# Converting the FFN weights in other places: four slices in attention, four in MoE, one engine step per f-step in the FFN

## The chip, the cores and the metric

The kernel runs on one core of one Trainium2 chip. The metric is the device time of one execution in microseconds (us), lower is better. The core has five engines that run their own instruction queues: TensorE (PE in the profile; PEld its weight loads), VectorE (DVE), ScalarE (ACT), GpSimd (POOL) and SyncE (SP), which here only issues transfers. ScalarE and GpSimd issue transfers too, from the same queue as their other work. Each queue is worked off in order: an instruction that waits holds everything behind it.

## The reference

Three layers run one after the other on 4 x 448 = 1792 tokens of width 768.

```python
# attention: 12 heads, head_dim 64, heads mixed before and after the softmax
scores = scale * np.matmul(q, k.transpose(0, 1, 3, 2))
scores = np.einsum('bhij,hg->bgij', scores, w_pre)
attn = softmax(scores)
attn = np.einsum('bhij,hg->bgij', attn, w_post)
x = np.matmul(attn, v)            # to (1792, 768)
# MoE: 8 experts, top 1, w1[e] is 768 x 1024, w2[e] is 1024 x 768
out[mask] = gate_w[mask, None] * (np.maximum(x[mask] @ w1[e], 0.0) @ w2[e])
# FFN: w_in is 768 x 2048, w_out is 2048 x 768, both float64
h = x @ w_in
y = (h * (1.0 / (1.0 + np.exp(-h)))) @ w_out
```

The FFN's weights arrive as float64. [...]

## The kernel before

**Float32 by parts.** Every large operand is split into a rounded part and a rest (`rhi`, `rlo` for weights, `xhi`, `xlo` and the like for activations; `split`, `wsplit`). ScalarE casts the first, VectorE subtracts for the second. Three matmuls (`mm3`, lines 798 to 800) then make one product. The split weights live in a ring of four pairs.

**Conversion.** The weights of the FFN are cut into 16 slices (`f`), each 128 x 1536 wide: 768 columns of `w_in`, 768 of `w_out`. A chunk of a slice is loaded as pairs of 32-bit words into a tile `D` and turned into float32 in a tile `CM` in five VectorE operations (mask the high word, add the low word, put in the sign, take out the exponent, multiply) and two ScalarE operations; then `CM` is stored to `w_d[f]` in device memory. The FFN loads slices from there. In attention, slices 0 to 7 are converted, in 48 chunks of 256 columns; in the FFN's first half slices 8 to 15, in 16 chunks of 768 columns.

**Attention** is ordered by a planner (`Plan`): each operation has a due time, a cost and the engines it may run on; a list scheduler writes one queue per engine. Chunk n of the conversion is due at an even share of the 180 groups (lines 648 to 657). SyncE issues all loads, the relay transfers `G<-S` and the conversion's transfers.

**MoE** runs 18 slots of 128 tokens (`slots`). A slot has four matmul steps: two `mm1` (18 matmuls of 512 columns each) and two `mm2` (24 of 384), interleaved with the slot before, so there are 72 steps. Each step splits two weight pairs (`rhi`, `rlo<-wraw`), two steps ahead of TensorE. At a slot's end ScalarE evicts `y` and GpSimd scatters it to `y_d`. `hook(s)` is called with s = a + 2 after slot a; for s = 12, 13, 14 it loads the three x tiles of the FFN's first token group (`xload`), on ScalarE's queue, and for s = 13, 14, 15 it transposes them (`fT`, two calls each).

**FFN.** Five token groups (four of 384 tokens, one of 256), and twice (for slices 0 to 7, then 8 to 15) all groups: 80 f-steps. In f-step n: `s1` (h of one slice; sigmoid on ScalarE, the product `sg` on VectorE, split into `gh`, `gl`), the transposes of the next group's x, `s2` of the f-step before (adds into six PSUM banks), the split of the slice two steps ahead, the load of the slice four ahead, and the conversion. After a group's last slice, `s2` copies the banks into tiles `ob` (two buffers for three tiles of a group) and GpSimd stores them to `p_d`. The next group's x is loaded at its predecessor's first f-step and transposed from the second on. The loads of slices and the conversion's transfers are SyncE's.

In the FFN's conversion a chunk has five steps, one per f-step: load; mask and first ScalarE operation; add and sign; exponent and second ScalarE operation; multiply and store. `D` and `CM` have two buffers; chunk n begins at f-step n x 36 // 16.

Of the kernel before, what the change touches and what calls it, by code (L numbers as in the profile page):

```python
# [9 lines left out]
F32 = mybir.dt.float32  # L10
F32R = mybir.dt.float32r
I32 = mybir.dt.int32
# [19 lines left out]
FH = NF // 2  # L32

# [194 lines left out]
def attention(tc, nc, q, k, v, x_d, oh, cum, zsum, c_e8, ident, wp1, wp2, wg_sb, wf, w_d, bias_e, bias_1):  # L228
    with ExitStack() as st:
# [573 lines left out]
def experts(tc, nc, x_d, y_d, w1, w2, wf, w_d, p_d, bias_e, bias_1, out, ident, oh, cum, zsum, consts,  # L803
# [6 lines left out]
    with outer:  # L810
# [115 lines left out]
        CC = DM  # L926
        wv = wf.bitcast(I32)

        def convert(n, step):
            f, c = FH + n // 2, n % 2 * CC  # L930
            V, A = nc.vector, nc.scalar
            if step == 0:
                tiles["D", n] = gpool.tile([128, CC, 2], I32, name="D", tag="D")
                nc.sync.dma_start(out=tiles["D", n].rearrange("p a b -> p (a b)"), in_=wv[f, :, 2 * c:2 * (c + CC)])
                return
            d = tiles["D", n]
            low, high = d[:, :, 0], d[:, :, 1]
            if step == 1:
                tiles["CM", n] = gpool.tile([128, CC], I32, name="CM", tag="CM")
            m = tiles["CM", n]  # L940
            fl = m.bitcast(F32)
            if step == 1:
                V.tensor_scalar(out=m, in0=high, scalar1=0xfffff, scalar2=None, op0=ALU.bitwise_and)
                A.activation(out=fl, in_=m, func=ACTF.Identity, scale=2.0 ** -20, bias=bias_1)  # L944
            elif step == 2:
                V.scalar_tensor_tensor(out=fl, in0=low.bitcast(U32), scalar=2.0 ** -52, in1=fl, op0=ALU.mult, op1=ALU.add)  # L946
                V.scalar_tensor_tensor(out=m, in0=high, scalar=-(1 << 31), in1=m, op0=ALU.bitwise_and, op1=ALU.bitwise_or)
            elif step == 3:
                V.tensor_scalar(out=high, in0=high, scalar1=20, scalar2=0x7ff,  # L949
                                op0=ALU.logical_shift_right, op1=ALU.bitwise_and)  # L950
                A.activation(out=high, in_=high, func=ACTF.Relu, scale=2.0 ** 23, bias=bias_e)
            elif step == 4:
                V.tensor_tensor(out=fl, in0=fl, in1=high.bitcast(F32), op=ALU.mult)  # L953
                nc.sync.dma_start(out=w_d[f][:, c:c + CC], in_=fl)
# [247 lines left out]
```

## Time and profile before

| | us |
|---|---|
| median of 3 runs (1488.95 to 1495.48) | 1491.22 |
| the profiled execution | 1493.94 |
| its span in the trace | 1492.2 |
| attention, 45 to 555 | 510 |
| MoE, 571 to 945 | 374 |
| FFN, first half with conversion, 945 to 1245.8 | 300.8 |
| FFN, second half, 1245.8 to 1480 | 234.2 |

Busy over the whole span: TensorE 1354.8 us (91%), VectorE 1101.2 (74%), ScalarE 875.8 (59%), GpSimd 507.8 (34%). Such a share is an average over stages with different limits, so the stages are read apart. The granted clock (PEclk) is TensorE's share of full speed in a stretch, 1.00 being 2.4 GHz and 0.50 being 1.2 GHz. In a timeline, `[0.57 <-ACT rhi]` behind a row is the idle time of that engine ahead of the instruction and what ended it. A queue name with q (ACTq, SPq) is the engine's sequencer, which issues transfers.

### The profile page before, as it was taken

What the parts mean: (1) busy time and instruction counts of PE and PEld (TensorE: products, weight loads), DVE (VectorE), ACT (ScalarE), POOL (GpSimd) and SP (SyncE); (2) the same over time, 40 slices, a digit from 0 to 9 for tenths busy, and PEclk for the clock granted to TensorE, in tenths of its full rate; (3) what the DMA queues carried; (4) which work ended last, traced back from release to release, by engine and by line L of the source; (5) the groups of instructions that cost most, each with busy time, mean ns of one, the idle gap of its engine ahead of it and who ended that gap; (6) DMA issues with size and microseconds to landing.
All of it is one profiled execution on the core that took longest, in us unless ns stands there. A gap on an engine that the chain in (4) does not pass through costs nothing. (4 is left out here: it accounts for less than half of the span.)

```text
span 1492.2 us, 24452 instructions
## 1 busy us (share of the span) xinstructions
PE 1354.8 (91%) x8838; PEld 1222.8 (82%) x8838; DVE 1101.2 (74%) x1652; ACT 875.8 (59%) x1500; POOL 507.8 (34%) x613
## 2 busy tenths in 40 slices
PE   4898989899899988999999999898898969999997
PEld 2777878777787877888887889797797959999996
DVE  5999879999898867797887788466566655445554
ACT  3766667777667645777887687444354444343332
POOL 7988668778867742141111110000000000000000
PEclk8999999999999998999999999898999999999998
DMA  7545554654554462179436740555555555355533
GB/s 226 174 154 169 175 171 153 206 179 165 163 166 155 139 200 93 30 268 334 148 121 233 260 154 22 189 189 196 207 188 203 178 203 212 127 190 191 188 132 116
DMA packets 110252, 259.85 MB, mean 174 GB/s; under 512 B 9308, under 2 KB 64896, under 8 KB 110128
## 3 DMA queue, kind: packets, MB, share of 16 engines
q1 hardware_dynamic: 101600, 223.38, 44.9%
q0 software_dynamic: 6512, 29.37, 5.6%
q10 hardware_dynamic: 2016, 5.51, 1.1%
q8 instruction: 71, 1.16, 0.3%
q14 instruction: 53, 0.43, 0.1%
HBM read 254.28 MB, written 36.18 MB: 195 GB/s over the span
## 5 line engine op out<-in xcount | busy, mean ns | idle before, releaser
L850 DVE TENSOR_TENSOR rlo<-wraw,rhi 128x1536 fp32r<-128x1536 f32 x144 | 246.7, 1756 | 63.3 <-ACT rhi L849 62.3
L849 ACT CAST rhi<-wraw 128x1536 fp32r<-128x1536 f32 x144 | 205.0, 1476 | 9.5 <-DMA wraw<-in_moe_w_dram 9.4
L363 POOL TENSOR_TENSOR GL<-G,GH 120x448 fp32r<-120x448 f32 (+1 forms) x164 | 202.3, 1242 | 15.8 <-PE m L799 5.8
L425 PEld LDWEIGHTS m<-WM,E 120*112 120x112 f32 (+1 forms) x1440 | 172.8, 181 | 34.1 <-POOL WM L412 10.2
L425 PE MATMUL m<-WM,E 120*112 120x120 f32 (+1 forms) x1440 | 183.5, 273 | 16.0 <-DVE a_sb L255 5.4
L856 DVE TENSOR_TENSOR rlo<-wf,rhi 128x1536 fp32r<-128x1536 f32 x80 | 140.6, 1758 | 69.3 <-ACT rhi L855 69.3
L798 PE MATMUL b<-fxhi,rhi 128*128 128x384 f32 (+1 forms) x480 | 161.4, 336 | 23.6 <-DVE sg L983 14.6
L800 PE MATMUL b<-fxhi,rlo 128*128 128x384 f32 (+1 forms) x480 | 161.2, 336 | 7.2 <-DVE rlo L856 7.2
L799 PE MATMUL b<-fxlo,rhi 128*128 128x384 f32 (+1 forms) x480 | 160.0, 333 | 0.0
L798 PE MATMUL b<-rhi,gh 128*128 128x384 f32 x436 | 151.0, 346 | 7.6 <-ACT gh L855 4.6
L800 PE MATMUL b<-rhi,gl 128*128 128x384 f32 x436 | 148.6, 341 | 0.0
L799 PE MATMUL b<-rlo,gh 128*128 128x384 f32 x436 | 148.1, 340 | 0.0
L391 ACT ACTIVATE E<-m,mx 120x448 f32<-120x448 f32 x180 | 114.2, 635 | 51.2 <-DVE mx L381 30.0
L381 DVE TENSOR_REDUCE mx<-m 120x1 f32<-120x448 f32 x180 | 109.9, 615 | 18.7 <-PE m L800 18.0
L855 ACT CAST rhi<-wf 128x1536 fp32r<-128x1536 f32 x80 | 118.1, 1478 | 2.0 <-issue 1.3
L798 PEld LDWEIGHTS b<-fxhi,rhi 128*128 128x128 f32 x480 | 93.9, 196 | 25.8 <-DVE sg L983 16.1
L981 ACT ACTIVATE sg<-b 128x384 f32<-128x384 f32 (+1 forms) x80 | 37.2, 465 | 131.4 <-PE b L800 131.3
L906 POOL DMA_INDIRECT y_d<-y,idx_s x18 | 18.3, 1018 | 280.3 <-ACT y L904 244.4
L1012 POOL DMA_DIRECT2D p_d<-ob x14 | 7.7, 550 | 306.1 <-DVE ob L1011 298.8
L983 DVE TENSOR_TENSOR sg<-b,sg 128x384 f32<-128x384 f32 (+1 forms) x80 | 42.3, 529 | 89.5 <-ACT sg L981 89.3
L328 PE MATMUL qkp<-kh,qs 128*120 128x448 f32 (+1 forms) x192 | 84.2, 439 | 23.6 <-DVE qs L319 21.3
L800 PEld LDWEIGHTS b<-fxhi,rlo 128*128 128x128 f32 x480 | 93.8, 195 | 10.0 <-DVE rlo L856 9.8
(196 smaller groups left out, 3420.4 us busy)
## 6 DMA issues: line engine op xcount, KB each, us to landing
wraw<-in_moe_w_dram SPq DMA_DIRECT2D x76, 1536.0 KB
wf<-w_d SPq DMA_DIRECT2D x80, 768.0 KB
G<-S SPq DMA_DIRECT2D x176, 210.0 KB
D<-in_wf_dram SPq DMA_DIRECT2D x48, 256.0 KB
D<-in_wf_dram SPq DMA_DIRECT2D x16, 768.0 KB
rawq<-in_q_dram SPq DMA_DIRECT2D x32, 360.0 KB
raw<-in_k_dram SPq DMA_DIRECT2D x36, 224.0 KB
w_d<-CM SPq DMA_DIRECT2D x48, 128.0 KB
```

Source lines behind the costliest of these rows:

```text
L328: nc.tensor.matmul(p[:m, :S], qs, kh, start=True, stop=False)
L363: G.tensor_tensor(out=t[:n], in0=x[:n], in1=hi[:n].bitcast(F32), op=ALU.subtract)
L381: V.tensor_reduce(out=mx[:n], in_=tiles["m1", i, g][:n, :S], axis=AX.X, op=ALU.max, negate=True)
L391: A.activation(out=t[:n], in_=tiles.pop(("m1", i, g))[:n, :S], func=ACTF.Exp, bias=tiles.pop(("mx", i, g))[:n], accum_out=tiles["z", i, g ...
L425: nc.tensor.matmul(p[:, c, :, :nr], x[:n, c * CH:(c + 1) * CH], wm[:n, :, :nr], start=True, stop=True)
L798: nc.tensor.matmul(p, lh, rh, start=first, stop=False)
L799: nc.tensor.matmul(p, lh, rl, start=False, stop=False)
L800: nc.tensor.matmul(p, ll, rh, start=False, stop=last)
L849: nc.scalar.copy(hi, src)
L850: nc.vector.tensor_tensor(out=lo, in0=src, in1=hi.bitcast(F32), op=ALU.subtract)
L855: nc.scalar.copy(hi, src)
L856: nc.vector.tensor_tensor(out=lo, in0=src, in1=hi.bitcast(F32), op=ALU.subtract)
```

## The change

- Attention converts slices 0 to 3 (`FA = 4`): 24 chunks of 256 columns instead of 48.
- MoE converts slices 4 to 7 with a new class `Convert`: 16 chunks of 384 columns, from matmul step 24 on, chunk n beginning n x 42 // 16 steps later.
- The FFN converts slices 8 to 15 with the same class: 16 chunks of 768 columns, chunk n beginning at f-step n x 36 // 16 as before. A chunk now has the load and five further steps, in each of which only one engine works on it: VectorE, ScalarE, VectorE twice, ScalarE, VectorE twice and the store. `D` and `CM` still have two buffers.
- Loads and stores of `Convert` are issued by GpSimd, not SyncE.
- `ob` has three buffers.
- x of a group is loaded a group ahead: group 1's tiles in MoE (s = 16, 17, 18), the others at the last slice of the group two before.

```diff
+FA = 4
-        for f in range(FH):
+        for f in range(FA):
...
+            def tick(self):
+                for x in list(self.live):
+                    x[0] += 1
+                    self.step(*x)
+                    if x[0] == 5:
+                        self.live.remove(x)
+                while self.begun < len(self.chunks) and self.starts[self.begun] <= self.time:
+                    f, c = self.chunks[self.begun]
+                    d = self.pool.tile([128, self.cols, 2], I32, name="D", tag="D", bufs=2)
+                    m = self.pool.tile([128, self.cols], I32, name="CM", tag="CM", bufs=2)
+                    nc.gpsimd.dma_start(out=d.rearrange("p a b -> p (a b)"), in_=wv[f, :, 2 * c:2 * (c + self.cols)])
+                    self.live.append([0, f, c, d, m])
+                    self.begun += 1
+                self.time += 1
...
+                if k == 1:
+                    V.tensor_scalar(out=m, in0=high, scalar1=0xfffff, scalar2=None, op0=ALU.bitwise_and)
+                elif k == 2:
+                    A.activation(out=fl, in_=m, func=ACTF.Identity, scale=2.0 ** -20, bias=bias_1)
+                elif k == 3:
+                    V.scalar_tensor_tensor(out=fl, in0=low.bitcast(U32), scalar=2.0 ** -52, in1=fl, op0=ALU.mult, op1=ALU.add)
+                    V.tensor_scalar(out=low, in0=high, scalar1=20, scalar2=0x7ff,
...
+                elif k == 4:
+                    A.activation(out=low, in_=low, func=ACTF.Relu, scale=2.0 ** 23, bias=bias_e)
+                else:
+                    V.tensor_tensor(out=fl, in0=fl, in1=low.bitcast(F32), op=ALU.mult)
+                    V.scalar_tensor_tensor(out=m, in0=high, scalar=-(1 << 31), in1=m, op0=ALU.bitwise_and, op1=ALU.bitwise_or)
+                    nc.gpsimd.dma_start(out=w_d[f][:, c:c + self.cols], in_=fl)
...
-                    ob = gpool.tile([128, DM], F32, name="ob", tag="ob")
+                    ob = gpool.tile([128, DM], F32, name="ob", tag="ob", bufs=3)
...
+                if 4 <= j < 7:
+                    xload(1, j - 4)
+            conv = Convert(wr, FA, FH, 384, 4 * NS0 - 30)
+            def tick(n):
+                if n >= 24:
+                    conv.tick()
+            slots(0, NS0, hook, tick)
...
+            conv = Convert(gpool, FH, NF, DM, len(work) // 2 - 4)
...
-                    if f == 0:
-                        for j in range(nj):
-                            xload(nxt, j)
+                    if f == FH - 1 and nxt + 1 < len(fgroups):
+                        for j in range(fgroups[nxt + 1][1] // 128):
+                            xload(nxt + 1, j)
...
+                conv.tick()
```

**VectorE in MoE.** One slot of four steps in the queue before: `rlo` are the weight splits, `xlo` and `hlo` the rests of the next activations.

```order
L850 TENSOR_TENSOR rlo<-wraw_7498,rhi 128x1536 x2
L856 TENSOR_TENSOR xlo<-b_9130,xhi 128x384
L856 TENSOR_TENSOR xlo<-b_9136,xhi 128x384
L850 TENSOR_TENSOR rlo<-wraw_7500,rhi 128x1536 x2
L856 TENSOR_TENSOR hlo<-b_9180,hhi 128x512
L850 TENSOR_TENSOR rlo<-wraw_7499,rhi 128x1536 x2
L850 TENSOR_TENSOR rlo<-wraw_7501,rhi 128x1536 x2
```

One slot of it now, from the seventh slot on. Lines 958 to 969 are the conversion.

```order
L851 TENSOR_TENSOR rlo<-wraw_7234,rhi 128x1536 x2
L857 TENSOR_TENSOR xlo<-b_9681,xhi 128x384
L857 TENSOR_TENSOR xlo<-b_9687,xhi 128x384
L968 TENSOR_TENSOR CM<-CM,D 128x384
L969 SCALAR_TENSOR_TENSOR CM<-D,CM 128x384
L851 TENSOR_TENSOR rlo<-wraw_7236,rhi 128x1536 x2
L857 TENSOR_TENSOR hlo<-b_9735,hhi 128x512
L962 SCALAR_TENSOR_TENSOR CM<-D,CM 128x384
L963 TENSOR_SCALAR D<-D 128x384
L851 TENSOR_TENSOR rlo<-wraw_7235,rhi 128x1536 x2
L958 TENSOR_SCALAR CM<-D 128x384
L851 TENSOR_TENSOR rlo<-wraw_7237,rhi 128x1536 x2
```

Five conversion operations now stand between the weight splits of this slot.

**VectorE in the FFN, first half.** One f-step in the queue before, from a weight split to the next product, with what each waits for (DMAHW and DMASW are transfers that SyncE or ScalarE, and that GpSimd issued).

```order
L856 TENSOR_TENSOR rlo<-wf,rhi 128x1536 [waits DMAHW5_49,Activation_49]
L953 TENSOR_TENSOR CM<-CM,D 128x768
L946 SCALAR_TENSOR_TENSOR CM<-D,CM 128x768
L947 SCALAR_TENSOR_TENSOR CM<-D,CM 128x768 [waits DVE_49]
L983 TENSOR_TENSOR sg<-b_11951,sg 128x384 [waits Activation_49]
```

The same f-step (the sixth) now.

```order
L857 TENSOR_TENSOR rlo<-wf,rhi 128x1536 [waits DMAHW5_49,Activation_49]
L968 TENSOR_TENSOR CM<-CM,D 128x768
L969 SCALAR_TENSOR_TENSOR CM<-D,CM 128x768 [waits DVE_49]
L962 SCALAR_TENSOR_TENSOR CM<-D,CM 128x768
L963 TENSOR_SCALAR D<-D 128x768 [waits DVE_49]
L958 TENSOR_SCALAR CM<-D 128x768 [waits DMASW4_49,DMASW3_49]
L999 TENSOR_TENSOR sg<-b_11921,sg 128x384 [waits Activation_49]
```

Lines 968 and 969 finish chunk 0, 962 and 963 are chunk 1, and 958 begins chunk 2 in the buffers of chunk 0; it stands ahead of the product `sg` and waits for two of GpSimd's transfers.

**GpSimd in the FFN, first half.** Its queue before held the stores of `ob` alone.

```order
L1012 DMA p_d_78<-ob 128x768
L1012 DMA p_d_79<-ob 128x768
L1012 DMA p_d_80<-ob 128x768
L1012 DMA p_d_81<-ob 128x768
L1012 DMA p_d_82<-ob 128x768
```

Its start now, up to the first group's stores.

```order
L948 DMA D<-in_wf_dram 128x1536 [waits DMASW1_49,DVE_49,DMASW2_49,PE_49,Activation_49]
L948 DMA D<-in_wf_dram 128x1536 [waits PE_49]
L948 DMA D<-in_wf_dram 128x1536 [waits DMASW1_49,DMASW3_49,DVE_49,Activation_49]
L970 DMA w_d_70<-CM 128x768 [waits DMASW4_49]
L948 DMA D<-in_wf_dram 128x1536 [waits DMASW2_49,DMASW5_49,DVE_49,Activation_49]
L970 DMA w_d_70<-CM 128x768 [waits DMASW6_49]
L1028 DMA p_d_78<-ob 128x768 [waits DVE_49,Activation_49]
```

The third load (chunk 2) stands ahead of the store of chunk 0 and waits for VectorE; the store itself waits for VectorE no more, since the load in front of it has done so.

## Rows read from the trace of the kernel before

**Rows 1.** Windows, four stages: busy us (instructions) of PE, PEld, DVE, ACT, POOL, clock, DMA.

```profile
45.00:555.00 510.00, 470.94 (x3974) 398.70 (x3974) 457.28 (x929) 351.88 (x854) 381.09 (x495) 0.98 0.54 167
571.00:945.00 374.00, 357.91 (x1862) 316.82 (x1862) 298.51 (x251) 278.00 (x299) 66.53 (x41) 0.97 0.48 165
945.00:1245.80 300.80, 258.04 (x1448) 250.02 (x1447) 185.00 (x234) 133.91 (x187) 6.58 (x12) 0.93 0.55 196
1245.80:1480.00 234.20, 231.74 (x1377) 230.87 (x1376) 122.11 (x147) 91.79 (x120) 13.32 (x15) 1.00 0.47 169
```

**Rows 2.** Windows of the tile D (conversion) alone: DVE, ACT, POOL busy, clock, DMA.

```profile
45.00:555.00 510.00, 115.69 (x201) 24.40 (x46) 23.85 (x29) 0.98 0.54 167
945.00:1245.80 300.80, 61.24 (x80) 16.06 (x16) 0.00 (x0) 0.93 0.55 196
```

**Rows 3.** Waits of TensorE in attention, 45 to 555: us, times, longest.

```profile
PE m L799 <- POOL GL L363: 11.6, 9, 3.8
PE qkp L329 <- DVE kl L306: 5.4, 5, 2.0
PE m L425 <- DVE a_sb L255: 5.4, 5, 2.5
```

**Rows 4.** Windows of single MoE slots, scatter to scatter: plain, then three with x loads.

```profile
729.33:748.10 18.77, 18.52 (x99) 16.43 (x98) 15.84 (x13) 15.07 (x17) 3.43 (x3) 1.00 0.63 211
804.43:829.01 24.58, 21.90 (x100) 18.51 (x99) 15.76 (x13) 14.95 (x17) 3.42 (x2) 0.86 0.87 305
829.01:848.53 19.52, 19.13 (x104) 17.14 (x104) 16.77 (x15) 15.83 (x19) 3.42 (x2) 1.00 0.60 203
848.53:870.24 21.71, 19.66 (x104) 17.19 (x104) 16.69 (x15) 15.72 (x19) 3.43 (x3) 1.00 0.64 215
```

**Rows 5.** Timeline of VectorE in the plain slot: start, us, line, tiles, idle before.

```profile
730.45 3.43 DVE L850 TENSOR_TENSOR rlo<-wraw,rhi 128x1536 fp32r<-128x1536 f32 x2 [0.45 <-ACT rhi L849]
733.79 0.68 DVE L856 TENSOR_TENSOR hlo<-b,hhi 128x512 fp32r<-128x512 f32 x1
735.62 3.43 DVE L850 TENSOR_TENSOR rlo<-wraw,rhi 128x1536 fp32r<-128x1536 f32 x2 [1.14 <-ACT rhi L849]
...
747.76 1.01 DVE L856 TENSOR_TENSOR xlo<-b,xhi 128x384 fp32r<-128x384 f32 x2
```

**Rows 6.** Timeline of ScalarE at the first x load in MoE.

```profile
812.50 0.60 ACT L886 ACTIVATE h<-b 128x512 f32<-128x512 f32 x1 [5.12 <-DMA y_d<-y,idx_s]
```

**Rows 7.** Instructions of tiles p_d and xg: issue ns min/median/max; p_d's time to landing.

```profile
L1012 POOL DMA_DIRECT2D p_d<-ob x14: 542/542/602, 1005.9 to 1249.7; - x14
...
DMA to landing us min/median/max: 2.6/3.5/7.6
L860 POOL DMA_INDIRECT xg<-x_d,idx_g x18: 947/2405/2612, 571.4 to 871.6; - x18
```

**Rows 8.** Waits of TensorE in the FFN's first half, the two largest of six.

```profile
PE b L798 <- DVE sg L983: 14.6, 3, 5.0
PE b L965 <- DMA x<-y_d: 10.9, 4, 4.8
```

**Rows 9.** Timeline of VectorE in one f-step of the first half.

```profile
1083.58 0.56 DVE L983 TENSOR_TENSOR sg<-b,sg 128x384 f32<-128x384 f32 x1 [1.77 <-ACT sg L981]
...
1086.46 1.76 DVE L856 TENSOR_TENSOR rlo<-wf,rhi 128x1536 fp32r<-128x1536 f32 x1 [0.72 <-ACT rhi L855]
1088.14 0.95 DVE L953 TENSOR_TENSOR CM<-CM,D 128x768 f32<-128x768 f32 x1
1089.01 0.95 DVE L946 SCALAR_TENSOR_TENSOR CM<-D,CM 128x768 f32<-128x768 uint32 x1
1089.99 0.96 DVE L947 SCALAR_TENSOR_TENSOR CM<-D,CM 128x768 int32<-128x768 int32 x1
```

**Rows 10.** Windows of 5 us at the first group end: busy, clock as in rows 1.

```profile
1015.00:1020.00 5.00, 2.43 (x8) 2.43 (x9) 3.66 (x7) 2.26 (x3) 0.00 (x0) 0.50 0.76 273
1020.00:1025.00 5.00, 5.00 (x21) 4.90 (x20) 2.64 (x3) 1.65 (x3) 0.00 (x0) 0.62 0.75 275
```

More of the change, by code (lines that the diff above doesn't have):

```diff
@@ L924, in pload @@
             tiles["fp", gi, j] = x
-        CC = DM
         wv = wf.bitcast(I32)
[L929 to L954, printed above, removed]
@@ new lines, in experts, with __init__, step @@
+        class Convert:
+            def __init__(self, pool, f0, f1, cols, steps):
+                self.pool, self.cols = pool, cols
+                self.chunks = [(f, c) for f in range(f0, f1) for c in range(0, 2 * DM, cols)]
+                self.starts = [n * steps // len(self.chunks) for n in range(len(self.chunks))]
+                self.time, self.begun, self.live = 0, 0, []
+            def tick(self):
[12 more added lines that the diff above has]
+                self.time += 1
+            def step(self, k, f, c, d, m):
+                V, A = nc.vector, nc.scalar
+                low, high = d[:, :, 0], d[:, :, 1]
+                fl = m.bitcast(F32)
+                if k == 1:
[5 more added lines that the diff above has]
+                    V.tensor_scalar(out=low, in0=high, scalar1=20, scalar2=0x7ff,
+                                    op0=ALU.logical_shift_right, op1=ALU.bitwise_and)
+                elif k == 4:
[4 more added lines that the diff above has]
+                    nc.gpsimd.dma_start(out=w_d[f][:, c:c + self.cols], in_=fl)
@@ L1075, in slots @@
                     hook(a + 2)
+                tick(n)
         with tc.manual_schedule():
@@ L1107, in hook @@
                     xload(0, j)
-            slots(0, NS0, hook)
+                if 4 <= j < 7:
[5 more added lines that the diff above has]
+            slots(0, NS0, hook, tick)
+            assert not conv.live and conv.begun == len(conv.chunks)
             total = nc.values_load(es_i[0:1, 2 * NS:2 * NS + 1], min_val=0, max_val=NS)
@@ L1120, in experts @@
             gpool = outer.enter_context(tc.tile_pool(name="gpool", bufs=2, side="right", reuse_waits="tile"))
-            NC = 2 * (NF - FH)
-            begin = {(n * (len(work) // 2 - 4)) // NC: n for n in range(NC)}
-            stage = {}
+            conv = Convert(gpool, FH, NF, DM, len(work) // 2 - 4)
             for n, (gi, f) in enumerate(work):
@@ L1142, in experts @@
                     fload(n + 4)
-                for c, t in list(stage.items()):
-                    convert(c, t)
-                    stage[c] = t + 1
-                    if t == 4:
-                        del stage[c]
-                if n in begin:
-                    convert(begin[n], 0)
-                    stage[begin[n]] = 1
+                conv.tick()
             for j in range(fgroups[-1][1] // 128):
```

2 lines of the change are left out of this document (1 added, 1 removed).

## Prediction

> **What bounds the kernel now.** I read the busy times by stage first, then in each stage what TensorE waits for, then the timelines of the engines named there. The stages [rows 1] are attention (510 us), MoE (374 us), the FFN's first half (300.8 us, its conversion inside) and its second half (234.2 us). TensorE's busy share is highest everywhere, but the slack differs. The second half is TensorE alone: busy 231.74 of 234.2 us, clock 1.00. The first half does the same matmuls plus 22 groups of three transposes and takes 66.6 us longer, with 258.04 busy at clock 0.93: this is where most can be won. In attention TensorE is idle for 39.1 us, and VectorE is busy for 457.28 of 510 us. In MoE TensorE is nearly full: a plain slot takes 18.77 us with 18.52 busy, and VectorE is busy for 15.84 of it [rows 4].
>
> The profiled execution took 1493.94 us, 2.7 us over the median of the three runs (1491.22); I sum against the former and take 2.7 off.
>
> **Attention loses half its conversion.** 46 of the 48 chunks lie in 45 to 555 us and cost VectorE 115.69 us there [rows 2], 2.52 us each, so 24 fewer free 60 us; VectorE's share falls from 90% to 78%. It is not the bound, so this is no gain of 60. TensorE's largest waits [rows 3] are 11.6 us on GpSimd and 5.4 + 5.4 = 10.8 us on VectorE. I take the VectorE waits as the gain, **-11 us**. Bounds: all idle time and the clock's 2% at most (49 us; I use 30, as the GpSimd waits have a cover of their own), and +5 the other way, since the planner orders everything anew with the same costs. SyncE loses 48 transfer issues, and the relay transfers behind them can only start earlier.
>
> **MoE gains 16 chunks of 384 columns.** They start at matmul step 24 of 72 and spread over 42 steps: 16/42 x 4 = 1.52 chunks in a slot.
> - VectorE's work: no such chunk is in the trace. A 768-wide one costs 61.24/16 = 3.83 us [rows 2], half of it 1.91; a 256-wide one amid attention 2.52. I take 2.1, near the first, because MoE's own VectorE work runs alone. Per slot 1.52 x 2.1 = 3.2 us against 18.77 - 15.84 = 2.93 us of idle time. The idle pieces are short, 0.45 to 1.14 us in front of the weight splits [rows 5], so the splits come late and TensorE follows. 0.27 us over 10.5 slots: +3 (ends 0 and +10). ScalarE has 3.70 us free in a slot [rows 4] for two operations a chunk of about 0.5 us each (half of 16.06/16 [rows 2]), 1.5 us, so it isn't the bound.
> - Loads that a buffer holds back: D has two buffers and a chunk lives five steps, so in 11 of 14 cases the load waits for the last VectorE operation of the chunk two before, behind that chunk's store on GpSimd's queue, and VectorE reads it one step later. The nearest transfer is the 384 KB store p_d: issue 0.54, landing 2.6 / 3.5 / 7.6 us [rows 7]. Store issue, gap and landing make 0.9 + 3.5 = 4.4 us; VectorE comes back after 3.43 + 0.68 or 1.01, 4.1 to 4.4 us [rows 5]. At the median nothing is lost, at 7.6 us 4.1. I take 0.8 us x 11 = +9 (0 to +45), since MoE's weight loads fill the DMA engines in about half the slots. Behind the waiting VectorE stand the weight splits, and behind them TensorE.
> - Loads of x moved: group 1's three loads go to ScalarE's queue after slots 14 to 16. Such a load waits until the last y scatter has landed, and ScalarE stands with it: 5.12 us in one place [rows 6]. The three slots with such a load took 24.58, 19.52 and 21.71 us [rows 4]. The last two hold 0.77 us of transposes, so the cost over 18.77 is 5.8, 0 and 2.2, a mean of 2.7. Two new ones cost +5 (0 to +12); after the third no weight split is left to be late.
> MoE in all: **+17 us** (+2 to +45).
>
> **FFN first half: what is won.** Its floor is the second half's 234.2 plus 22 x 0.385 of transposes, 242.7 us; so 58 us lie above it, 42.5 of waits (the sum of the six entries of TensorE's list, the two largest in [rows 8]) and the rest clock. The third eviction tile removes the wait for the p_d store that holds ScalarE and VectorE at the group ends (14.6 us on TensorE); x a group ahead removes 10.9 us. One engine step per f-step removes ScalarE's waits for VectorE, which delayed the splits.
>
> **What the FFN gets instead.** A chunk now lives one step longer, its tiles still have two buffers, and the starts are 36/16 = 2.25 steps apart. So in 8 of 14 chunks the first operation stands in the same f-step, and on VectorE's queue directly behind, the last operations of the chunk two before it; the load between them can only be issued when those are done (the order rows show it). VectorE then stands for the landing, less the two operations between. By the timeline [rows 9]: from the product sg (time 0) conversion begins at 4.56, its last two operations end at 6.41; with a landing of 4.8 us (between p_d's 3.5 and 7.6, since this load is twice as large) the blocked operation ends at 11.9. The next product should start at 6.65 (a step of 234.2/37.3 = 6.27 plus 0.39): it is 5.2 us late. TensorE has s2 of one step and s1 of the next in front of it, which covers about 5.2. The second blocked step of a pair comes two steps later; by then 5.2 - 2.1 = 3.1 us are left over, so it is 8.3 late and TensorE loses 3.1. At the landing's ends this is 0.5 and 8.7. After idle spells of about 5 us the granted clock stood at 0.50 and 0.62 in the next two stretches of 5 us [rows 10], half-rate time worth 4.4 us; for 3 us I take 2. Three pairs: 3 x 5 = 15 (2 to 35). The fourth lies in the group of 256 tokens, where a step is only 4.2 us: late 7.1 then 9.6 against a cover of 2.8, 11 + 4 of clock = 15 (8 to 25). With 4 left at group ends: 58 - 34 = **-24 us** (-48 to +2). The stores behind the waiting loads on GpSimd's queue, p_d among them, come later too, which costs nothing with three tiles. SyncE no longer holds the wf loads behind a w_d store; no row shows TensorE waiting for those.
>
> Sum: -11 + 17 - 24 = -18; 1493.94 - 18 - 2.7 = 1473 us.
>
> GpSimd issued most of MoE's gathers in 2.4 us and the quickest in 0.95 [rows 7]. The Trainium skill, SBUF — State Buffer, "Who interferes with whom", says that VectorE's two-port modes lock GpSimd out of the shared pair, which starves the descriptors of transfers that GpSimd issues. The long gathers agree; but the same section holds that TENSOR_TENSOR, most of MoE's work, doesn't block descriptor writing, and that the rows do not settle. This is the third rival below. The skill's DMA: Bandwidth & Descriptors, "Anatomy of one DMA", gives about 2.0 us + bytes/436e3: 3.8 us for a 768 KB load as an estimate, for which the FFN's pairs would cost some 6 us less.
>
> **Rivals.**
> 1. The loads land fast (3.5 us) everywhere: FFN -42, MoE +6, attention -20: 1491 - 56 = 1435. For it: VectorE is under two thirds busy in the FFN [rows 1]. Against: half the stage's 300 us have other transfers running.
> 2. Nothing in sum: attention's TensorE waits pass to GpSimd (already its largest, 11.6), 0; MoE +25; FFN -24: about 1492.
> 3. Slower: GpSimd issues the conversion's loads in 2.4 us instead of 0.54, as it did the gathers beside VectorE [rows 7]. Each load on the path lands 1.9 us later: MoE 11 x 1.9 = 21 more; in the FFN a pair becomes late 7.1 and 10.2, 7 us of wait and 4 of clock, 33 for three, and 21 for the last: FFN 0. Sum -11 + 38 + 0 = +27: about 1518. It decides from a landing of about 6.5 us on. The loads that the trace shows were SyncE's, so this is open.
> 4. Slower by landing alone (7.6 us, p_d's longest): MoE +45, FFN +2, attention -11: 1491 + 36 = 1527.
> That the change doesn't do what it says is no rival: the order shows 24, 16 and 16 chunks.
>
> **How the numbers follow.** Forecast 0.45, rival 1 0.15, rival 2 0.17, rival 3 0.14, rival 4 0.09. About 0.5% (7.5 us) is what a measurement of this kernel can tell from no change. Faster: 0.40 of the forecast, rival 1, 0.03 of rival 2: 0.58. Same: 0.05 + 0.11 + 0.02 = 0.18. Slower: 0.24, rivals 3 and 4 and a rest of rival 2. The range runs from 1440 (half of rival 1) to 1512 (short of most of rivals 3 and 4). The forecast's own range is 1455 to 1490.
>
> **What would show it.** Right: TensorE's waits for x<-y_d and at group ends gone; VectorE waiting for a DMA at L958 in the FFN, eight times, in pairs; MoE slots from the sixth on at 19 to 21 us with VectorE above 95%; two more places where ScalarE waits for the y scatter; attention some 10 us shorter. Wrong: MoE slots still at 18.8 us, or no wait at L958 (then rival 1); D loads landing after more than 6.5 us (3 or 4); attention longer by the new order.

## The result and the profile after

The changed kernel takes 1510.9 us (median of 4 runs, 1505.5 to 1516.9) against 1490.6 before: 1.013 times the time before, 95% interval 1.010 to 1.016. I had forecast 1473, faster. The profiled execution took 1509.5 us with a span of 1507.7, 15.5 more than before.

The four stages of the changed kernel, in windows with the columns of [rows 1] (busy us of PE, PEld, DVE, ACT, POOL, clock, DMA):

```profile
45.00:540.00 495.00, 466.04 (x3971) 400.95 (x3971) 424.45 (x866) 323.11 (x782) 343.18 (x458) 0.98 0.49 156
556.00:950.10 394.10, 361.77 (x1860) 316.70 (x1859) 330.46 (x330) 294.52 (x330) 80.90 (x75) 0.97 0.54 184
950.10:1267.15 317.05, 263.15 (x1450) 257.10 (x1450) 185.76 (x233) 133.66 (x186) 23.08 (x42) 0.90 0.54 182
1267.15:1495.00 227.85, 227.66 (x1356) 227.19 (x1355) 121.99 (x144) 91.64 (x121) 15.69 (x14) 1.00 0.50 174
```

Beside [rows 1], attention is 15 us shorter (forecast 11), MoE 20 longer (forecast 17) and the FFN's first half 16 longer, where I had forecast 24 shorter. From there to the end of the span it is 5.8 us shorter (246.4 to 240.6), for which I had forecast nothing. So the FFN's first half misses by 40 us, more than the sum does (33); the other stages together bring 7 back. Its clock fell from 0.93 to 0.90 and TensorE is idle for 53.9 of 317 us.

What TensorE and VectorE wait for there (950 to 1267: us in total, times, longest); it answers to [rows 8]:

```profile
PE b L799 <- DVE sg L999: 26.1, 7, 10.8
PE b L799 <- ACT gh L856: 20.1, 4, 10.9
PE b L981 <- DVE sg L999: 6.8, 2, 3.4
...
DVE CM L958 <- DMA w_d<-CM: 49.5, 8, 8.5
...
DVE CM L958 <- DMA D<-in_wf_dram: 10.3, 6, 3.0
```

TensorE's waits of [rows 8] for x are gone, and of those at the group ends 0.4 us for an eviction tile is left, as the prediction said. In their place TensorE waits for the product `sg` and what follows from it (`gh`), 53 us. VectorE, which makes `sg`, stands at L958, the first operation of a chunk: eight long waits, the number forecast.

VectorE's timeline at the first of them, and GpSimd's (start, us, line, tiles, idle before):

```profile
985.83 0.96 DVE L969 SCALAR_TENSOR_TENSOR CM<-D,CM 128x768 int32<-128x768 int32 x1
986.70 0.95 DVE L962 SCALAR_TENSOR_TENSOR CM<-D,CM 128x768 f32<-128x768 uint32 x1
987.69 0.56 DVE L963 TENSOR_SCALAR D<-D 128x768 int32<-128x768 int32 x1
993.65 0.56 DVE L958 TENSOR_SCALAR CM<-D 128x768 int32<-128x768 int32 x1 [5.40 <-DMA w_d<-CM]
994.12 0.55 DVE L999 TENSOR_TENSOR sg<-b,sg 128x384 f32<-128x384 f32 x1
...
987.33 0.54 POOL L948 DMA_DIRECT2D D<-in_wf_dram  x1 [40.10 <-ACT sg L997]
987.87 0.55 POOL L970 DMA_DIRECT2D w_d<-CM  x1
```

L969 ends chunk 0. Then GpSimd issues the load for chunk 2, and behind it chunk 0's store; L958 needs both, the load for `D` and the store for the buffer of `CM`. It comes to its place at 988.25 and starts at 993.65; `sg`, on which TensorE waits, stands right behind. At 994.73 TensorE starts again after 5.02 us of idle time.

At two of the eight places a group's three eviction stores stand on GpSimd's queue between the load and the store, and the wait is 8.4 us instead of 5.4:

```profile
1083.99 0.53 POOL L948 DMA_DIRECT2D D<-in_wf_dram  x1 [19.11 <-issue]
1084.51 1.63 POOL L1028 DMA_DIRECT2D p_d<-ob  x3
1086.13 0.54 POOL L970 DMA_DIRECT2D w_d<-CM  x1
...
1093.29 0.56 DVE L958 TENSOR_SCALAR CM<-D 128x768 int32<-128x768 int32 x1 [8.38 <-DMA w_d<-CM]
...
1094.37 0.69 PE L799 MATMUL b<-fxhi,rhi 128*128 128x384 f32 x1 [10.83 <-DVE sg L999]
```

### The profile page after: what moved, and what is told of

It reads as the page before. It is cut to its first block, busy times and chain, and to the rows that moved or that the text cites. A ratio compares the mean times of both kernels' runs of the same rounds, so it can differ in the third digit from the quotient of the medians.

```text
span 1507.7 us, 24340 instructions
## 1 busy us (share of the span) xinstructions
PE 1357.1 (90%) x8838; PEld 1231.1 (82%) x8838; DVE 1103.2 (73%) x1671; ACT 863.5 (57%) x1461; POOL 504.2 (33%) x641
## 5 line engine op out<-in xcount | busy, mean ns | idle before, releaser
L364 POOL TENSOR_TENSOR GL<-G,GH 120x448 fp32r<-120x448 f32 (+1 forms) x137 | 164.7, 1210 | 22.0 <-PE m L800 8.0
L856 ACT CAST gh<-sg 128x384 fp32r<-128x384 f32 (+1 forms) x77 | 38.2, 496 | 156.9 <-DVE sg L999 156.9
L970 POOL DMA_DIRECT2D w_d<-CM x32 | 18.5, 577 | 280.4 <-DVE CM L969 256.7
L413 POOL TENSOR_SCALAR WM<-wp,rz 120x120 f32<-120x120 f32 x180 | 88.8, 501 | 47.4 <-PE m L426 21.7
L799 PEld LDWEIGHTS b<-rhi,gh 128*128 128x128 f32 x436 | 84.9, 195 | 22.0 <-ACT gh L856 21.0
```

Of the source, the lines that this page charges most:

```text
L364: G.tensor_tensor(out=t[:n], in0=x[:n], in1=hi[:n].bitcast(F32), op=ALU.subtract)
L413: G.tensor_scalar(out=wm[:n], in0=wp2[:n], scalar1=rz, scalar2=1.0, op0=ALU.mult, op1=ALU.mult)
L799: nc.tensor.matmul(p, lh, rh, start=first, stop=False)
L856: nc.scalar.copy(hi, src)
```

## Experiments

For a table by stage I take three marks from each timeline: the routing's first instruction of line 712 (711 before), the first sigmoid of the FFN and the 41st, which begins the second half. "MoE" is from the first mark to the second and so holds the routing too.

| kernel | first mark, at | MoE | FFN, first half | median |
|---|---|---|---|---|
| before | 565.6 | 379.2 | 301.0 | 1490.6 |
| changed | 550.6 | 399.5 | 317.0 | 1510.9 |
| FFN chunks 2.5 steps apart | 551.9 | 400.4 | 268.5 | 1461.2 |
| third buffer of CM | 550.5 | 398.9 | 301.4 | 1494.4 |
| nothing converted in MoE | 565.4 | 377.4 | 316.5 | 1499.8 |
| MoE's transfers on SyncE | 549.6 | 393.2 | 315.0 | 1500.3 |
| MoE's chunks spread | 548.5 | 393.1 | 318.6 | 1502.6 |
| groups 2 to 4 without transposes | 552.9 | 400.0 | 309.1 | 1504.4 |
| 2.5 steps, nothing in MoE | 564.1 | 376.8 | 263.3 | 1445.5 |
| 2.5 steps, MoE spread and on SyncE | 549.6 | 406.2 | 267.8 | 1464.6 |
| four D, nothing in MoE | 567.1 | 376.5 | 252.5 | 1437.4 |
| two tiles, x late, nothing in MoE | 565.2 | 380.5 | 294.0 | 1480.2 |
| four D, MoE loads 2 steps ahead | 549.3 | 396.5 | 254.7 | 1442.0 |
| the same, MoE spread | 551.3 | 386.8 | 253.1 | 1433.3 |
| the same, spread and on SyncE | 548.8 | 390.1 | 253.4 | 1432.5 |
| the same, on SyncE alone | 552.3 | 396.1 | 252.3 | 1440.8 |

Kernels with the same MoE differ there by some 1.5 us between executions.

### The FFN's chunks 2.5 f-steps apart

```diff
-            conv = Convert(gpool, FH, NF, DM, len(work) // 2 - 4)
+            conv = Convert(gpool, FH, NF, DM, len(work) // 2)
```

> The FFN's 16 chunks begin 40/16 = 2.5 f-steps apart instead of 36/16 = 2.25, nothing else: the chunk two ahead then always begins in the f-step in which its predecessor ends, so its first operation (L958) stands one whole f-step behind the load, never in the same one. Theory reuse (the buffers held one step longer make VectorE stand for the load and the store, 59.8 us in 13 waits in the changed kernel): those waits go, the FFN's first half falls from 317 to 245 to 258 us, and the whole from 1510.9 to 1440 to 1456. Rival load (the conversion's work on VectorE and ScalarE or its transfers slow the f-steps, wherever the chunks begin): the first half stays above 300 and the whole above 1495. Attention and MoE stay at 495 and 394 by either.

1461.2 us, 0.980 of before (0.975 to 0.984). The first half fell by 48.5 us, with the same operations, the same bytes and the same two buffers (the last two chunks now end a few f-steps into the second half, which gets no longer by it). So it was the reuse and not the load of the conversion. It fell by less than I had forecast for this run (to 245 to 258 us), and its waits show why:

```profile
PE b L799 <- ACT gh L856: 7.5, 6, 3.4
PE b L799 <- DVE sg L999: 7.0, 7, 2.2
PE b L801 <- DVE rlo L857: 3.3, 6, 1.3
...
DVE CM L958 <- DMA D<-in_wf_dram: 22.0, 14, 2.9
```

The long waits are gone, but now all 14 reused chunks wait up to 2.9 us. The load stands behind the store on GpSimd's queue and lands 6.3 to 6.8 us after its issue (in the three loads whose landing the trace tells), and L958's place comes sooner: in the first case the load is issued at 989.8 and VectorE begins to wait at 994.96. A whole f-step between them is not enough.

The clock is part of the 48.5 us. The first half of this kernel:

```profile
952.30:1220.76 268.46, 250.78 (x1460) 243.39 (x1458) 181.81 (x228) 132.25 (x185) 22.73 (x40) 0.99 0.62 213
```

TensorE is busy for 250.8 us here and for 263.2 in the changed kernel, with the same matmuls, at clock 0.99 against 0.90: 12.4 us. The other 36 are idle time.

### A third buffer of CM alone

```diff
-  m = self.pool.tile([128, self.cols], I32, name="CM", tag="CM", bufs=2)
+  m = self.pool.tile([128, self.cols], I32, name="CM", tag="CM", bufs=2 if self.cols < DM else 3)
```

> In the FFN alone the tile CM gets a third buffer, D keeps two. VectorE at L958 then waits for the load of D and no longer for the store of the chunk two before, which stands behind that load on GpSimd's queue. Theory load is enough (D lands after 5.3 to 5.9 us, the store some 0.5 us later): the 49.5 us put down to w_d<-CM turn into about 45 put down to D<-in_wf; the FFN's first half falls by 0 to 6 us from 317, the whole stays at 1504 to 1511. Rival store (it is the store behind the load that costs): the waits at L958 fall to under 25 us in sum, the first half to about 290 us, the whole to 1480 to 1490.

1494.4 us, 1.002 (1.000 to 1.005), the first half 15.6 us shorter: between the two theories. The waits came out nearer to the first, the time nearer to the second. VectorE's waits at L958 come to

```profile
DVE CM L958 <- DMA D<-in_wf_dram: 45.5, 14, 4.7
```

instead of 59.8. The eight long ones are now 4.2 to 4.7 us, all for the load. So the store behind the load cost about 1 us at six places and 3.8 at the two where eviction stores stood in between; the load itself is the larger part.

### Four buffers of D, and the load ahead of the stores

Here 24 chunks of 512 columns stand in the place of 16 of 768, over the same 40 f-steps (the last of them end just behind), and a load is issued ahead of the stores of its f-step. Slices 4 to 7 are converted in attention, so that MoE is out of the way.

```diff
-FA = 4
+FA = FH
...
+                self.starts = [min(n * steps // len(self.chunks), steps - 3) for n in range(len(self.chunks))]
...
+                fresh = []
                 while self.begun < len(self.chunks) and self.starts[self.begun] <= self.time:
...
+                    fresh.append([1 - self.lead, f, c, d, None])
...
+                self.live += fresh
...
+            conv = Convert(gpool, FH, NF, 512, len(work) // 2, 4, 3, 1)
```

> As the version with 2.5 f-steps between chunks and no conversion in MoE (1445.5 us, first half 263.3 us), with the FFN's conversion in 24 chunks of 512 columns, 40/24 f-steps apart, four buffers of D and three of CM, and the load issued ahead of the f-step's stores: no load waits for VectorE in the same step any more. Theory (VectorE's remaining waits for D at L958, 22.0 us in 14 places with 2.5 steps between chunks, still delay the product): they fall to under 6 us, the first half to 250 to 257 us, the whole to 1432 to 1440. Rival (what is left over the floor of 242.7 us is the group ends and VectorE's own work): first half 260 or more, whole 1442 to 1450.

1437.4 us, 0.966 (0.962 to 0.971). The wait for `D` is gone altogether; 3.4 us for `CM` are left in three places. The first half takes 252.5 us, 10 over the floor of 242.7 that the prediction worked out. From the second f-step to the end of the fourth group an f-step takes 5.2 to 6.9 us, most of them 6.6, which is the floor's step with its transposes (6.27 + 0.39). So what is over the floor lies in the fifth group: its eight steps of 256 tokens take 48.9 us, where 8 x 4.2 would be 33. The floor is itself not the least that is possible, since the second half from which it was taken held some 4 us of waits for eviction tiles (next section).

### The third eviction tile and the early x, undone

On the version with 2.5 f-steps and nothing converted in MoE:

```diff
-                    ob = gpool.tile([128, DM], F32, name="ob", tag="ob", bufs=3)
+                    ob = gpool.tile([128, DM], F32, name="ob", tag="ob")
...
-                if 4 <= j < 7:
-                    xload(1, j - 4)
...
+                    if f == 0:
+                        for j in range(nj):
+                            xload(nxt, j)
...
-                    if f == FH - 1 and nxt + 1 < len(fgroups):
-                        for j in range(fgroups[nxt + 1][1] // 128):
-                            xload(nxt + 1, j)
```

> As the version with 2.5 f-steps between chunks and no conversion in MoE (1445.5 us), with two eviction tiles instead of three and x loaded at its predecessor's first f-step, as the kernel before does. Theory (the two edits are worth the TensorE waits that the kernel before shows for them, 14.6 and 10.9 us, less about nothing for the x loads in MoE): 1465 to 1473, the first half 285 to 292. Rival (those waits lay in the shadow of others): under 1456.

1480.2 us against 1445.5; the first half 294.0 against 263.3. The two edits are worth 31 us there, 5 more than the waits in [rows 8] (25.5) and more than either theory had. TensorE waits for x again, 8.8 us in four places. No run takes the two edits apart. The time from the 41st sigmoid to the last also goes back, from 225.9 to 230.2 us, near the 229.8 of before: in the second half, too, two eviction tiles cost 4 us. The prediction had nothing for that.

### Transposes left out

```diff
-            x = tiles["fxT", gi]
+            x = tiles["fxT", min(gi, 1)]
...
-                    if 1 <= f <= 2 * nj:
+                    if nxt == 1 and 1 <= f <= 2 * nj:
```

> Left out: the transposes and splits of x for the token groups 2 to 4 in the FFN, which reuse group 1's; the output is not the reference's. Theory bank (the transposes share two PSUM banks with the product h, so in a step with transposes the next step's first matmul needs a bank that the delayed product sg has not yet read, and TensorE has only s2, 3.1 us, to do while VectorE stands): where the transposes are gone TensorE's idle time at a blocked step falls by about 2 to 3 us (10.83 to 7 to 9, 3.39 to 0 to 1.5, 6.86 to 4 to 5.5), while the one in group 0, which keeps them, stays at 5.0. With 16 transpose steps of 0.39 us gone as well, the first half falls from 317 to 300 to 306 us and the whole to 1494 to 1500. Rival (TensorE's cover is the same with and without transposes): those idle times stay within 1 us, the first half falls by 6 us alone, to 309 to 312.

This asked why TensorE found so little to do while VectorE stood. In a step with transposes these take the second of two PSUM banks, so the next step's first matmul waits for a bank that `sg` hasn't read. Without them two idle times fell by 2 to 3 us (10.83 to 8.80, 6.86 to 3.78), but two others rose by as much (2.86 to 5.22, 3.39 to 5.88) and two by some 0.9 (3.38 to 4.33, 6.00 to 6.93). The first half fell by 7.9 us, near what the transposes themselves cost (16 x 0.39 = 6.2). So the banks only decide where TensorE stands, not for how long in sum: the theory that they are the cause falls.

### Attention's gain and MoE's loss

Nothing converted in MoE, with the changed kernel's FFN, and then with 2.5 f-steps between its chunks:

```diff
-FA = 4
+FA = FH
```

> Slices 4 to 7 are converted in attention again (FA = 8), none in MoE; the FFN is the changed one. Theory trade (attention's gain of 15 us is the 24 chunks gone, and of MoE's loss of 20 us about 15 is conversion): attention takes about 510 us again, MoE 376 to 382 (the two x loads more remain), and the whole is 1506 to 1514, as far as the measurement goes the same. Rival order (attention's gain comes from SyncE's queue or a new order, MoE's loss from the x loads and the clock): attention stays under 502 or MoE above 388.

> Both edits tried alone, together: the FFN's chunks begin 2.5 f-steps apart, and slices 4 to 7 are converted in attention, none in MoE. If the parts add up: 1461.2 + 15 (attention) - 22 (MoE) = 1454, 1449 to 1459. Rival (the parts don't add, since the stage boundaries hide some of each): 1460 or more.

1499.8 us (1.005, interval 1.002 to 1.008) and 1445.5 us (0.970, 0.968 to 0.972). Both are below what I expected (1506 to 1514 and 1449 to 1459). The parts add up, and a little more: the FFN's first half of the second takes 263.3 us, and 268.5 and 267.8 with the same FFN behind a MoE that converts; why, no run shows. Attention takes back 14.8 us and MoE gives back 22.1. So attention's gain is the 24 chunks, and MoE's loss is the 16 chunks alone. The x loads moved into MoE cost nothing by themselves: MoE with them but without conversion takes 377.4 us, against 379.2 before.

### What the chunks cost in MoE

A store of the conversion that waits for VectorE stands ahead of the y scatter on GpSimd's queue. An example in the changed kernel, ScalarE's rows and GpSimd's:

```profile
793.02 0.56 ACT L905 ACTIVATE y<-b,gate_s 128x384 f32<-128x384 f32 x1
...
804.69 0.34 ACTq L919 DMA_DIRECT2D x<-y_d  x1
805.08 0.60 ACT L887 ACTIVATE h<-b 128x512 f32<-128x512 f32 x1 [8.27 <-DMA y_d<-y,idx_s]
...
798.09 0.55 POOL L970 DMA_DIRECT2D w_d<-CM  x1 [12.23 <-DVE CM L969]
798.95 1.43 POOL L907 DMA_INDIRECT y_d<-y,idx_s  x1 [0.31 <-issue]
```

`y` is complete at 793.6, its scatter goes out at 798.95, and ScalarE, which has an x load to issue behind the scatter's landing, stands until 805. The prediction didn't see that queue. Two single changes to MoE, and both together:

```diff
+            def __init__(self, pool, f0, f1, cols, steps, q=nc.gpsimd):
...
+                    self.q.dma_start(out=d.rearrange("p a b -> p (a b)"), in_=wv[f, :, 2 * c:2 * (c + self.cols)])
...
+            conv = Convert(wr, FA, FH, 384, 4 * NS0 - 30, nc.sync)
```

> In MoE alone, SyncE issues the conversion's loads and stores instead of GpSimd; the FFN's stay on GpSimd. Theory held scatter (on GpSimd's queue the y scatter stands behind a store of the conversion that waits for VectorE's last operation, and behind the scatter the x loads and with them ScalarE): ScalarE's waits for y_d in MoE, 28 us in 6 waits, fall to 11 to 16; MoE goes from 394 to 382 to 388 and the whole to 1499 to 1505. Rival VectorE (it has no idle time left, and the scatter's delay is covered): MoE stays at 390 to 396, the whole within 4 us of 1510.9. Rival weight loads (they stand behind the waiting stores on SyncE's queue): MoE above 400 and TensorE's waits for the weight splits longer.

```diff
-            conv = Convert(wr, FA, FH, 384, 4 * NS0 - 30)
+            conv = Convert(wr, FA, FH, 384, 4 * NS0 - 14)
...
-                if n >= 24:
+                if n >= 8:
```

> MoE's 16 conversion chunks begin at matmul step 8 instead of 24 and are 58/16 = 3.6 steps apart instead of 42/16 = 2.6; nothing else differs from the changed kernel. Without conversion MoE is 22 us shorter, and SyncE's queue for its transfers gives back 6 of them. Theory full VectorE (a chunk's operations take 2.37 us; at 1.52 chunks a slot they come to 3.6 us against 2.93 of idle time in a plain slot, at 1.10 chunks to 2.6): MoE falls from 399 to 385 to 389 us (from the routing's first line to the first sigmoid of the FFN), the whole from 1510.9 (1507.7 span) to 1497 to 1501. Rival chunk price (each chunk costs TensorE about 1 us wherever it stands, through the transfers or the two weight splits that it delays): MoE stays at 396 to 400.

Both edits together, with the FFN's chunks 2.5 steps apart:

> FFN chunks 2.5 f-steps apart; MoE chunks from step 8 on, 3.6 steps apart, their transfers on SyncE's queue. Theory: attention keeps its 15 us (495), MoE comes to 378 to 384 us, the FFN's first half stays at 268: 1439 to 1449 in all, under both kernels and under the version without conversion in MoE. Rival (what conversion costs in MoE is not VectorE's fill and not the held scatter): MoE 390 or more, the whole 1451 or more.

Each alone gave 6 us of MoE. The first is at the lower end of its theory (6 to 12). ScalarE's waits for `y_d` fell further than it said, from 28.0 to 3.1 us, but VectorE's waits for `D` rose from 7.0 to 15.0: one wait went and another came. The second is half of what its theory said. Both together lost 7 (MoE 406.2, 1464.6 us in all), which refutes my expectation. In the worst place of the combination VectorE's timeline has

```profile
684.75 0.36 DVE L958 TENSOR_SCALAR CM<-D 128x384 int32<-128x384 int32 x1 [9.89 <-DMA D<-in_wf_dram]
```

and the window over that wait, with the DMA engines' share and GB/s at its end,

```profile
675.00:685.00 10.00, 3.83 (x24) 3.48 (x22) 0.26 (x1) 2.47 (x4) 0.00 (x0) 0.84 1.03 392
```

On SyncE's queue the loads of `D` stand among MoE's weight loads, and the DMA engines are full in that window (1.03). VectorE waits for `D` for 31.3 us in nine places, against 7.0 in four in the changed kernel. So I took that wait out (four buffers of `D` in MoE, each load two matmul steps ahead) and tried the others again on top of the better FFN, with slices 4 to 7 in MoE again (`FA = 4`). Against the version with four `D` the call differs in:

```diff
-            conv = Convert(wr, FA, FH, 384, 4 * NS0 - 30, 2, 2, 1)
+            conv = Convert(wr, FA, FH, 384, 4 * NS0 - 30, 4, 2, 2)
```

> The same FFN, but slices 4 to 7 converted in MoE as in the changed kernel (from step 24, 2.6 steps apart, GpSimd's queue), with four buffers of D and each load issued two matmul steps ahead of its first operation instead of one. Theory landing (what conversion costs in MoE is VectorE standing for a D that lands 5 to 8 us after its issue amid the weight loads, most of all in the slots that load a new expert): MoE, 399.5 us in the changed kernel and 377.4 without conversion, comes to 380 to 388, and the whole is 5 to 12 us under the version without conversion in MoE. Rival fill (VectorE has no room for the operations, whenever D lands; or the y scatter behind the stores): MoE 393 or more, the whole equal to that version or longer.

The same with the spacing (`4 * NS0 - 14`, from step 8), with spacing and SyncE's queue, and with SyncE's queue alone:

> The version with loads two matmul steps ahead in MoE (MoE 396.5 us, 377 without conversion; no wait for D left), with MoE's chunks from step 8 on, 3.6 steps apart instead of 2.6, on GpSimd's queue. Theory fill (at 2.6 steps VectorE's own work in a slot is 15.84 + 3.6 us against 18.77; at 3.6 steps 15.84 + 2.6): MoE 380 to 387, the whole 1425 to 1433 against 1442.0. Rival queue (the y scatter and the x loads behind the stores on GpSimd's queue, and the clock after such a wait, are the larger part): MoE 391 or more.

> As the last, and MoE's conversion transfers on SyncE's queue. Theory fill and queue together: MoE 377 to 382, the whole 1420 to 1428, under the version without conversion in MoE (1437.4). Rival weight loads (SyncE's weight loads stand behind stores that wait for VectorE, and D's loads behind weight loads, as in the version with a lead of one step, where MoE took 406 us): MoE 391 or more.

> Loads two steps ahead, MoE's chunks from step 24 on and 2.6 steps apart as in the changed kernel, transfers on SyncE's queue. Theory queue alone: MoE 387 to 391 (fill is left). Rival fill alone: 394 to 398, as on GpSimd's queue. Rival weight loads: over 400.

The lead alone gave 3 us (396.5), though no wait for `D` is left (6.2 us for `CM` are): my landing theory falls. With the lead, spacing gives 10 (386.8), and the queue gives nothing (396.1; with the spacing 390.1). So of the 22 us that the chunks cost, some 10 go with the spacing, 3 with the waits for `D`, and 10 remain whose cause I can't name. The spacing edit also moves the chunks to other slots, and no run tells the two apart. That SyncE's queue gave 6 us with a lead of one step and none with two is left open.

Whether VectorE is simply full can be read more closely. A stretch of 190 us of the changed kernel's MoE, inside the part with chunks:

```profile
680.00:870.00 190.00, 174.18 (x891) 152.28 (x890) 166.10 (x171) 149.35 (x173) 36.63 (x42) 0.96 0.63 212
```

VectorE is busy for 87% of it, so it looks far from full. But the stretch is an average over unlike slots. Three plain slots of it, ahead of the first x load (the scatter that ends the second comes late, so the last two are read together):

```profile
714.58:733.69 19.11, 18.51 (x98) 16.45 (x98) 18.62 (x20) 16.14 (x19) 4.95 (x6) 1.00 0.80 257
733.69:756.54 22.85, 21.14 (x110) 18.62 (x110) 22.16 (x26) 20.15 (x23) 4.03 (x5) 1.00 0.64 208
756.54:772.43 15.89, 15.89 (x88) 14.26 (x86) 15.46 (x15) 13.19 (x16) 4.12 (x5) 1.00 0.31 96
```

Here VectorE is busy for 97% (56.24 of 57.85 us), and yet the slots are only 0.3, 0.5 and 0.7 us longer than with nothing converted, from one end of ScalarE's `y` to the next. So a full VectorE costs little where nothing else stands. Of the 22 us, 1.7 lie in a slot ahead of the first chunk and 19 in the nine stretches behind these slots. There ScalarE stands for y scatters at the x loads, and VectorE for `D`. At group 1's first x load it reads

```profile
895.90 0.60 ACT L887 ACTIVATE h<-b 128x512 f32<-128x512 f32 x1 [4.88 <-DMA y_d<-y,idx_s]
```

against 1.92 us of idle time with nothing converted, and that slot is 2.8 us longer. Which of these waits sets the time is not shown: with the transfers on SyncE's queue ScalarE's waits are nearly gone, and the longest of these slots are as long as before.

The version with the lead and the spacing takes 1433.3 us, 0.960 (0.958 to 0.963) of before, 78 us under the changed kernel. On SyncE's queue it is the same (1432.5, 0.960). Against the version without conversion in MoE (0.966, interval 0.962 to 0.971) it is ahead by less than the two intervals can tell apart.

## Why the prediction was wrong, step by step

**Attention, forecast -11, came out at -15.** Undoing the 24 chunks gives the 15 back, so the cause is right. The rows that I took the size from were the wrong ones. TensorE's waits in attention (45 to 540), the largest and the tiles of [rows 3]:

```profile
PE m L799 <- ACT E L392: 8.4, 6, 1.8
PE m L426 <- DVE a_sb L256: 8.0, 5, 2.6
PE m L800 <- POOL GL L364: 4.3, 2, 2.2
...
PE qkp L330 <- DVE kl L307: 1.8, 3, 1.2
```

The waits for VectorE hardly fell in sum (10.8 to 9.8); it was the wait for GpSimd that did (11.6 to 4.6 in both its lines), which I had left aside as covered otherwise, and a wait for ScalarE rose (3.0 to 8.4). TensorE's idle time fell by 10 us in all; that this is near the forecast's 11 is luck. Its busy time fell by another 5, for which the forecast had nothing. GpSimd's busy time fell by 38 us, of which 12 are the chunks' own operations; VectorE's share fell to 86%, not to the 78% that I had worked out, since the planner gave it other work.

**MoE, forecast +17, came out at +20, by terms that were each off.** I had 3 us for VectorE's work, 9 for held-back loads and 5 for the x loads. The runs show some 10 that go with the spacing, 3 for the loads, nothing for the x loads by themselves, and 10 without a name. So the sum came near by luck. Setting a slot's idle time (2.93 us) against its new work (3.2, measured 3.6) was right for the plain slots: they lose 0.3 to 0.7 us each, where the sum has 0.27. Wider spacing gave 10 us where this sum has 3, so what it saves must lie in the other slots. The signs I named agree for the plain slots with a chunk, 19.1 to 19.4 us with VectorE at 97%. The extra waits of ScalarE for the y scatter came from a store ahead of the scatter, which I had not looked for.

**FFN, forecast -24, came out at +16: the step that failed.** The mechanism stood in the prediction: eight blocked chunks in pairs, VectorE standing at L958, the load held until the chunk two before is done. The step that failed is the price of these chunks: 30 us in the sum (three pairs at 5 and one at 15), where taking the coincidence away gave 48.5. Of the three stage ranges this one alone (-48 to +2) does not hold the measurement. Three sizes were wrong.

- *The stall.* I took a landing of 4.8 us, which left 3.4 of stall. The load took 5.3 to 6.2 us (three loads tell), and the store behind it landed later still: 5.3 to 5.8 us of stall in six places, 8.4 and 8.5 in two. Of the eviction stores behind the load I wrote that they cost nothing with three tiles. They are themselves not waited for, but the chunk's store stands behind them, and that is the wait of 8.4.
- *The cover.* I gave TensorE 5.2 us of other work and so let the first of each pair cost nothing: 20.3 us of idle time for the eight, by the prediction's own figures. Measured, in order, 5.02, 3.38, 2.86, 10.83, 3.39, 6.86, 10.91 and 6.00, in sum 49.3 us, for stalls of 49.5 us in sum. The cover is no help in the sum. I put that down to the five conversion operations of a blocked step: from one `sg` to the next VectorE takes some 8.5 us even without the wait, against 6.6 of the step, and that uses up what cover there is. This is argued from the timeline; no run takes it apart. For the clock I had taken 10 us and the run shows 12.
- *The chunks that aren't blocked.* The sum has no price for the waits of the other six. A whole f-step lies between their load and L958, but the load goes out behind the store and takes about as long as the step: 10.3 us of waits in the changed kernel, 22.0 in the version with 2.5 steps. Smaller loads ahead of the stores, with more buffers, gave back 11 to 16 us (263.3 or 268.5 to 252.5).

Told by the runs' steps: of the 58 us over the floor that I had set down as won, 10 stay over it even in the best version and 16 lie between it and the version with 2.5 steps (268.5 - 252.5), the unblocked waits among them; so 32 are won, and 48.5 are lost to the blocked chunks (317.0 - 268.5): +16. Each term is a difference of two runs, so that the sum comes out proves nothing further. The third tile and the early x, for which I had 25.5, gave 31.

The load's row in the changed kernel's FFN (issue ns min/median/max) and its time to landing:

```profile
L948 POOL DMA_DIRECT2D D<-in_wf_dram x14: 531/542/757, 987.3 to 1237.0; - x14
...
DMA to landing us min/median/max: 5.3/5.9/6.2
```

The landing of 4.8 us lay between two rows for a transfer half as large. The Trainium skill's figure for a transfer, in DMA: Bandwidth & Descriptors, "Anatomy of one DMA" (2.0 us + bytes/436e3, by which a 768 KB load takes 3.8 us as an estimate), lies further off: measured 5.3 to 6.2 us beside the other transfers of this stage.

**The rivals.** The first (loads landing in 3.5 us everywhere) is refuted in the FFN by the landings above, and so is the second's condition, since attention's waits for GpSimd fell. GpSimd issuing the loads in 2.4 us (third rival) is refuted too: they took 0.53 to 0.76 us in the FFN and 0.55 to 0.63 in MoE, there all 16 beside a weight split of VectorE (TENSOR_TENSOR). This agrees with the sentence of the Trainium skill, SBUF — State Buffer, "Who interferes with whom", that TENSOR_TENSOR doesn't hold up descriptor writing, which the page marks as inferred. That this rival's 1518 lies near 1510.9 is chance. The fourth rival (a landing of 7.6 us, 1527) had the cause, a late landing, but most of its loss in MoE (+45) and 2 us in the FFN; the loads landed sooner than that, but a store stood behind them. The point from which I had let the sum turn to slower, a landing of about 6.5 us, is about what load and store took together in the changed kernel (issue at 987.33, L958 at 993.65).

## What to carry to other kernels

When a pipeline gets a step longer and keeps its buffers, count in how many cases the reuse falls into the same step as the release; those cases expose a whole transfer, and moving the starts by a quarter of a step is enough to avoid them. Price such a stall at its full length if the engine that stalls has a full queue in that step, and take the last transfer on the queue, not the one that the tile is named after. Before a transfer is moved to another engine's queue, list what stands behind it there: here a store that waits for VectorE came ahead of a scatter, and eviction stores came between a load and a store.

## What was not expected of the hardware

MoE's gathers of x, 2.4 us each in [rows 7] and in the versions with nothing converted in MoE, became shorter although VectorE had more to do:

```profile
L861 POOL DMA_INDIRECT xg<-x_d,idx_g x18: 943/1074/2607, 556.2 to 876.9; - x18
```

The median of the 18 is 1.07 us in the changed kernel, and 1.37 with loads two steps ahead. The traces show what the length goes with. Three gathers of the changed kernel:

```profile
678.15 2.40 POOL L861 DMA_INDIRECT xg<-x_d,idx_g  x1 [0.30 <-issue]
722.65 1.55 POOL L861 DMA_INDIRECT xg<-x_d,idx_g  x1 [0.30 <-issue]
735.16 1.06 POOL L861 DMA_INDIRECT xg<-x_d,idx_g  x1 [0.30 <-issue]
```

At the first a weight split on VectorE (`rlo`, TENSOR_TENSOR, 1.76 us) had begun 0.21 us earlier, at the second 1.08 us earlier, and each gather ends 0.85 to 0.87 us after its split does. At the third a conversion operation was just ending, and it takes 1.06. In the plain slot of [rows 5] the split begins at 730.45 and the gather, 2.40 us long, at 730.66. Over all 16 traces 171 gathers begin while a weight split runs. Of these, 167 end 0.82 to 0.94 us after that split, however long it still had to run; the other four begin within 0.02 us of its start and take 1.0 us. So the gathers became short where the conversion's operations moved the splits against them. My third rival was built on those 2.4 us, but the loads of the conversion, issued beside the same splits, take 0.6 us: the wait is the gather's and not the direct load's.
